# Padding four small tiles so that every operand on chip begins at a multiple of 128 bytes

## The chip, the cores and the metric

The kernel runs on one core of a Trainium2 chip. The metric is the device time of one execution in microseconds (us). A time for a kernel is the median of several executions. The profile is one further execution, recorded by the hardware profiler.

## The reference

```python
X = np.fft.rfft(x, axis=1)                    # x: 8 x 3008 x 256, float32
Yr = Xr @ w_r - Xi @ w_i + b_r                # 256 x 256 complex projection
Yi = Xr @ w_i + Xi @ w_r + b_i
Yr = np.sign(Yr) * np.maximum(np.abs(Yr) - 0.01, 0.0)      # and Yi the same
y = np.fft.irfft(Yr + 1j * Yi, n=3008, axis=1).astype(np.float32)
h = y.reshape(24064, 256) @ w_in              # 256 x 2048
out = np.maximum(0.01 * h, h) @ w_out         # 2048 x 256, result float32
```

Two parts follow each other: a spectral layer (Fourier transform, complex projection, soft threshold, inverse transform) and an MLP over 24064 tokens with a leaky ReLU between its two matrix products.

## The kernel before

**Transform.** The sequence length 3008 is 47 x 64, and the transform is done in two steps of matmuls, a 47-point one (`fwd`, `stage_a`, 120 partitions: 24 folded rows times 5 groups) and a 64-point one (`mid`, `stage_b`). Between them the data goes through a scratch tensor in HBM (`u_dram`), since the second step wants it in another layout. `proj` multiplies by the complex weights with three real products (`wr`, `wd`, `wn`), thresholds, and `stage_g` transforms back over 64 points. The result goes through HBM again (`v_dram`), and `inverse` does the last 47-point step with the constant `ga` and puts 512 tokens at a time into a tile `yc`.

**MLP.** 47 chunks `ci` of 512 tokens, and in each 8 steps `q` over the hidden width. The first product is done by Strassen's scheme with seven block products instead of eight: `forms` makes the seven token combinations (`yh`, `yl`, seven slots of 256 columns), and the weights' seven combinations lie in `win` (7 x 8 blocks of 128 columns). Each block product is three matmuls in float32r (`block`, L92), since every operand is split into a high and a low part: high x high, low x high, high x low. `moe_a` and `moe_b` combine the products in PSUM, apply the leaky ReLU into `gf`, and split that into `gh` and `gl`; `moe_o` (L576) makes the second product, 512 columns wide, from the stationary `wout` and the moving `gh`, `gl`.

The stationary operand of a matmul is loaded by a LDWEIGHTS, the moving one streams through. In L92 the stationary operand is `win` and the moving one `yh` or `yl`. In `proj` (L78) the stationary operand is the data `eh` and the moving one a weight (`wr`, `wd`, `wn`). In `stage_b` (L343) the data `u` is stationary and the constant `fb` moves; in `inverse` (L480) the data `vin` is stationary and the constant `ga` moves.

**Order.** A scheduler lays out the order of each engine. The transform of the next sequence is interleaved with the MLP of the present one at a pace that the code sets (`Stream`). Batch 0 and the loading of the weights form a start phase of about 170 us.

**Where tiles lie.** On chip memory has 224 KB in each partition. Tiles are placed one behind the other, constants first (`fb`, `sign`, then the pairs made by `pair`, then `bias`, `ga`), then the working tiles of the pool `sb` by their tag. A tile's start is thus the sum of the sizes ahead of it, rounded to 32 bytes. Added up for the kernel before:

| tile | first byte | its rest modulo 128 |
|---|---|---|
| `fb` | 1152 | 0 |
| `sign` (36 columns, 144 bytes) | 7552 | 0 |
| `win_hi`, `win_lo` | 7712, 36384 | 32 |
| `wr`, `wd`, `wn`, `gb` (hi and lo) | 65056 to 77856 | 32 |
| `fa0_hi`, `fa0_lo`, `fa1_hi`, `fa1_lo` (480 bytes each) | 78368 to 79808 | 32, 0, 96, 64 |
| `bias`, `ga`, `xi` (and `fa32`, 1440 bytes, in the same place) | 80288, 82336, 83360 | 32 |
| `yl`, `yh`, `gf`, `gl`, `gh`, `yc`, `wout`, `eh`, `zh`, `u`, `v`, `vin`, `xin`, `kc`, `t`, `ob` | 84800 to 220480 | 64 |
| `odd` (960 bytes) | 222528 | 64 |
| `p1`, `u2` | 223488, 224512, 225536 | 0 |

Slots inside the tiles of the MLP are 512 or 1024 bytes apart, so each operand of the MLP has the rest of its tile.

Of the kernel before, what the change touches and what calls it, by code (L numbers as in the profile page):

```python
# [8 lines left out]
F32 = mybir.dt.float32  # L9
F32R = mybir.dt.float32r  # L10
# [8 lines left out]
N1, N2, NK1 = 47, 64, 24  # L19
NG, NS = 5, 13  # L20
P = 128
PA = NK1 * NG
# [8 lines left out]
def spectral_mlp_kernel(  # L31
# [22 lines left out]
    NPAIR = NK1 // 2  # L54
# [8 lines left out]
    const = ctx.enter_context(tc.tile_pool(name="const", bufs=1))  # L63
    sb = ctx.enter_context(tc.tile_pool(name="sb", bufs=2))
# [4 lines left out]
    def bank(tag, bufs):  # L69
        return ps.tile([P, 512], F32, name=tag, tag=tag, bufs=bufs)  # L70
# [27 lines left out]
    consts = {}  # L98

    def pair(name, shape):  # L100
        consts[name] = tuple(const.tile(shape, F32R, name=f"{name}_{p}") for p in ("hi", "lo"))
        return consts[name]

    def load_plain(name, src, shape):
# [3 lines left out]
    def split_consts():  # L108
        for name in ("wr", "wd", "wn", "gb", "fa0", "fa1"):
            w = consts[name + "32"][0]  # L110
            hi, lo = pair(name, list(w.shape))
            act.copy(hi, w)
            dve.tensor_sub(lo, w, hi.bitcast(F32))
# [354 lines left out]
    def inverse(pi, eh):  # L468


        (_, _, n0), (_, _, n1) = pairs[pi]
        m = n0 + n1
        ne, n = m * NK1, m * N1
        vin = v_t[pi]
        py = bank("psf", 2)
        s = slice(eh * P, (eh + 1) * P)
        for c in range(2):
            for i in range(2):
                o = c * ne + i * n0 * NK1
                nc.tensor.matmul(py[:, o:o + P], vin[:, c, i, s], consts["ga"][:, c, :], start=True, stop=True)  # L480
        odd = sb.tile([P, 2 * NG * NK1], F32, name="odd", tag="odd", bufs=1)[:, :ne]
        y = sb.tile([P, NT], F32, name="y", tag="y")
        act.copy(odd, py[:, ne:2 * ne])
        dve.tensor_add(y[:, :ne], py[:, :ne], odd)
        ev, ov = (t.rearrange("p (m k) -> p m k", k=NK1)[:, :, 1:] for t in (py[:, :ne], odd))
        dve.tensor_sub(y[:, ne:n].rearrange("p (m k) -> p m k", m=m), ev, ov)
        lo = p0[pi]
        while lo < p0[pi + 1]:
            ci = lo // NT
            hi = min((ci + 1) * NT, p0[pi + 1])  # L490
            if ci not in f_t:
                f_t[ci] = sb.tile([P, NH, NT], F32, name="yc", tag="yc")
            act.copy(f_t[ci][:, eh, lo - ci * NT:hi - ci * NT], y[:, lo - p0[pi]:hi - p0[pi]])
            lo = hi
# [98 lines left out]
    def tokens(ci):  # L593

        yield
        for p in due[ci]:
            v_load(p)
            yield
        for _ in range(4 - len(due[ci])):
            yield  # L600
        for eh in range(NH):
            for p in due[ci]:
                inverse(p, eh)
                yield
        yield from forms(ci)
# [39 lines left out]
    FWD = NS * 6 * D  # L645


    fa32 = sb.tile([PA, 3, PA], F32, name="fa32", tag="xi", bufs=1)
    for h in range(2):
        sync.dma_start(fa32[:, h], fa[h])  # L650
    for h in range(3):
# [8 lines left out]
    for p in (0, 32):  # L660
        for r, src in enumerate((b_r, b_i)):
            sync.dma_start(brow[p:p + 1, r * D:(r + 1) * D], src.unsqueeze(0))
    sign = const.tile([P, NK1 + NPAIR], F32, name="sign")
    sync.dma_start(sign, sg)
    sync.dma_start(consts["gb32"][0], gb)

# [4 lines left out]
    f0.finish()  # L671
    load_win(1, (sync, sync), written[7])
    pair("win", [P, 7, NQ, P])
    win_tmp = (
        sb.tile([P, NH * NIN], F32, name="cva", tag="vin"), sb.tile([P, NH * NIN], F32, name="cvq", tag="gf"),
# [33 lines left out]
    for eh in range(NH):  # L709
        for p in due[0]:  # L710
            inverse(p, eh)
# [131 lines left out]
```

## Time and profile before

| | |
|---|---|
| time of the kernel, median of 3 runs | 2604.93 us (2601.47 to 2607.09) |
| time of the profiled execution | 2600.34 us |
| its span, first to last instruction | 2598.6 us |
| TensorE matmul busy | 2537.5 us (98%) |
| VectorE, ScalarE, GpSimd busy | 1897.1 us (73%), 1668.5 us (64%), 229.6 us (9%) |
| mean granted TensorE clock | 0.993 |

PE is TensorE's matmul stream, PEld its weight loads, DVE VectorE, ACT ScalarE, POOL GpSimd. Matmuls overlap each other in the records: a matmul with 256 columns is shown 280 ns long while the next one starts about 117 ns after it. So the pace of TensorE is read from the starts, and durations serve to compare like with like.

### The profile page before, as it was taken

To read this page: it belongs to the slowest core of one execution; us is meant where nothing else is said; L and a number is where in the kernel's file an instruction comes from. 1 tells how busy PE (TensorE), PEld (TensorE's weight loads), DVE (VectorE), ACT (ScalarE), POOL (GpSimd) and SP (SyncE) were. 2 spreads that over 40 slices of the span, in tenths; PEclk is the share of its full clock that TensorE was granted. 3 is DMA by queue.
4 is the path that set the end of the run, shared out by engine and by line. 5 is a ranking of instruction groups with operands and counts; after the bars stand their busy time and mean duration, and the time that the engine had idled before them with its cause. 6 is when DMAs were issued, how large, how long until landed. Compare 5 with 4: busy or idle time off the path is not lost.

```text
span 2598.6 us, 42643 instructions
## 1 busy us (share of the span) xinstructions
PE 2537.5 (98%) x16300; PEld 2281.5 (88%) x16300; DVE 1897.1 (73%) x3403; ACT 1668.5 (64%) x3174; POOL 229.6 (9%) x180
## 2 busy tenths in 40 slices
PE   5999999999999999999999999999999999999999
PEld 4689888999889998899988999889998889999998
DVE  7687786776777778777786777877777777767675
ACT  5766665776556666567665666566666667655564
POOL 0001121100110001100021000210002000000000
PEclk8999999999999999999999999999999999999999
DMA  8621132111221113211132111321113221101000
GB/s 259 179 85 50 48 89 72 54 47 48 82 78 49 45 41 90 75 55 51 33 97 68 49 49 37 104 67 49 49 36 101 64 58 48 44 17 32 9 17 17
DMA packets 119912, 165.13 MB, mean 64 GB/s; under 512 B 13601, under 2 KB 69917, under 8 KB 119709
## 3 DMA queue, kind: packets, MB, share of 16 engines
q1 hardware_dynamic: 79120, 115.55, 14.6%
q10 hardware_dynamic: 40589, 46.87, 7.1%
q8 instruction: 128, 2.10, 0.4%
q14 instruction: 75, 0.61, 0.1%
HBM read 86.60 MB, written 75.76 MB: 62 GB/s over the span
## 4 chain that ended last, share of the span: by engine, by line
PE 89%; DVE 3%; DMA 2%; ACT 1%; issue 0%; ACTq 0%; SPq 0%; DVEq 0%
PE pso L576 38%; PE psh L92 34%; PE psf L78 11%; PE psf L480 3%; PE psf L343 3%; DMA u<-u_dram 1%; DMA u_dram<-xin 1%; DVE yl L506 0%; DVE gl L563 0%; DMA raw<-w_out_dram 0%; DVE gf L557 0%; ACT gh L561 0%; DVE yt L511 0%; ACT gf L559 0%; DVE yc L512 0%
## 5 line engine op out<-in xcount | busy, mean ns | idle before, releaser
L92 PE MATMUL psh<-yh,win_hi 128*128 128x256 f32 x2632 | 752.3, 286 | 13.8 <-DVE gf L546 10.6
L92 PE MATMUL psh<-yl,win_hi 128*128 128x256 f32 x2632 | 738.3, 280 | 0.6 <-DVE yl L506 0.5
L92 PE MATMUL psh<-yh,win_lo 128*128 128x256 f32 x2632 | 737.9, 280 | 0.0
L576 PE MATMUL pso<-gh,wout_hi 128*128 128x512 f32 x1504 | 593.9, 395 | 0.0
L576 PE MATMUL pso<-gl,wout_hi 128*128 128x512 f32 x1504 | 591.1, 393 | 0.5 <-DVE gl L563 0.5
L576 PE MATMUL pso<-gh,wout_lo 128*128 128x512 f32 x1504 | 590.4, 393 | 0.0
L563 DVE TENSOR_TENSOR gl<-gf,gh 128x1024 fp32r<-128x1024 f32 x376 | 471.8, 1255 | 92.7 <-ACT gh L561 90.6
L92 PEld LDWEIGHTS psh<-yh,win_hi 128*128 128x128 f32 x2632 | 497.0, 189 | 30.7 <-DVE gf L546 15.4
L92 PEld LDWEIGHTS psh<-yl,win_hi 128*128 128x128 f32 x2632 | 497.0, 189 | 12.5 <-DVE yl L506 1.0
L92 PEld LDWEIGHTS psh<-yh,win_lo 128*128 128x128 f32 x2632 | 496.6, 189 | 0.2
L557 DVE TENSOR_TENSOR gf<-psh,u 128x512 f32<-128x512 f32 x376 | 259.1, 689 | 256.3 <-PE psh L92 255.1
L561 ACT CAST gh<-gf 128x1024 fp32r<-128x1024 f32 x376 | 396.4, 1054 | 7.1
L559 ACT ACTIVATE gf<-gf 128x768 f32<-128x768 f32 x376 | 320.0, 851 | 49.5 <-DVE gf L557 47.7
L576 PEld LDWEIGHTS pso<-gl,wout_hi 128*128 128x128 f32 x1504 | 282.5, 188 | 62.9 <-DVE gl L563 1.0
L576 PEld LDWEIGHTS pso<-gh,wout_hi 128*128 128x128 f32 x1504 | 283.1, 188 | 46.9 <-ACT gh L561 0.4
L576 PEld LDWEIGHTS pso<-gh,wout_lo 128*128 128x128 f32 x1504 | 282.9, 188 | 44.9
L556 ACT ACTIVATE gf<-psh 128x256 f32<-128x256 f32 x376 | 145.5, 387 | 266.6 <-PE psh L92 246.9
L542 ACT COPY p<-psh 128x256 f32<-128x256 f32 x376 | 140.1, 373 | 220.2 <-PE psh L92 219.1
L379 POOL TENSOR_TENSOR kb<-bias,kc 128x512 f32<-128x512 f32 x84 | 119.0, 1417 | 1530.6 <-ACT kc L376 1409.6
L543 DVE TENSOR_TENSOR u<-psh,p 128x256 f32<-128x256 f32 x376 | 158.6, 422 | 105.8 <-ACT p L542 103.5
L545 DVE TENSOR_TENSOR gf<-psh,u 128x256 f32<-128x256 f32 x376 | 159.3, 424 | 29.7 <-PE psh L92 2.0
L546 DVE TENSOR_TENSOR gf<-psh,gf 128x256 f32<-128x256 f32 x376 | 159.1, 423 | 9.0
(134 smaller groups left out, 3253.2 us busy)
## 6 DMA issues: line engine op xcount, KB each, us to landing
u<-u_dram SPq DMA_DIRECT2D x192, 128.0 KB, 2.7
v_dram<-v ACTq DMA_DIRECT2D x192, 128.0 KB, 2.4
out_dram<-ob SPq DMA_DIRECT2D x94, 256.0 KB, 2.1
vin<-v_dram SPq DMA_DIRECT2D x96, 240.0 KB, 3.5
xin<-x_dram SPq DMA_DIRECT2D x90, 240.0 KB, 3.0
u_dram<-xin ACTq DMA_DIRECT2D x72, 240.0 KB, 2.4
u_dram<-xin SPq DMA_DIRECT2D x24, 240.0 KB, 3.9
raw<-w_out_dram SPq DMA_DIRECT2D x8, 512.0 KB, 5.0
```

The source lines that it names most:

```text
L78: last = nc.tensor.matmul(dst, a, b, start=(i == 0), stop=(i == len(terms) - 1))
L92: mlp[:] = [nc.tensor.matmul(dst, a, b, start=start and i == 0, stop=i == 2, skip_group_check=True)]
L542: act.copy(p1, b1[:, lo])
L543: dve.tensor_add(u2, b1[:, hi], p1)
L545: dve.tensor_add(g[:, 3], b2[:, hi], u2)
L546: dve.tensor_add(g[:, 3], b2[:, lo], g[:, 3])
L556: act.activation(g[:, 0], b1[:, lo], AF.Prelu, alpha=SLOPE)
L557: dve.tensor_add(g[:, 1:3], b2.rearrange("p (k n) -> p k n", k=2), u2.unsqueeze(1).broadcast_to([P, 2, HT]))
L559: act.activation(g[:, 1:4], g[:, 1:4], AF.Prelu, alpha=SLOPE)
L561: cp = act.copy(gh, g)
L563: parted[:] = [cp, dve.tensor_sub(gl, g, gh.bitcast(F32))]
L576: mlp[:] = [nc.tensor.matmul(po, a[:, f, s], r[:, i], start=(f == 0 and j == 0), stop=(f == NF - 1 and j == 2),)]
```

## The change

Four tiles whose row is no multiple of 128 bytes are made longer, and the code uses only the first part of each: the split constants made by `pair` (of which only the four `fa` tiles change, from 120 to 128 columns), `odd` (240 to 256 columns), `fa32` (rows of 120 to rows of 128) and `sign` (36 to 64 columns).

```diff
     def pair(name, shape):
-        consts[name] = tuple(const.tile(shape, F32R, name=f"{name}_{p}") for p in ("hi", "lo"))
+        full = shape[:-1] + [-(-shape[-1] // 32) * 32]
+        consts[name] = tuple(
+            const.tile(full, F32R, name=f"{name}_{p}")[..., :shape[-1]] for p in ("hi", "lo"))
         return consts[name]
...
-        odd = sb.tile([P, 2 * NG * NK1], F32, name="odd", tag="odd", bufs=1)[:, :ne]
+        odd = sb.tile([P, 256], F32, name="odd", tag="odd", bufs=1)[:, :ne]
...
-    fa32 = sb.tile([PA, 3, PA], F32, name="fa32", tag="xi", bufs=1)
+    fa32 = sb.tile([PA, 3, P], F32, name="fa32", tag="xi", bufs=1)[:, :, :PA]
...
-    sign = const.tile([P, NK1 + NPAIR], F32, name="sign")
+    sign = const.tile([P, 64], F32, name="sign")[:, :NK1 + NPAIR]
```

Everything behind a lengthened tile moves up: `win` to `gb` by 96 bytes, `bias`, `ga` and `xi` by 224, the working tiles by 320, `p1` and `u2` by 384. Afterwards every tile that the code allocates begins at a multiple of 128 bytes, and all of them but `sign` at 128 bytes past a multiple of 512 (before: `win` 32, `yh`, `gh` and `wout` 320, `p1` and `u2` 256 past one). Instructions, their order on each of the five engines and their semaphore waits are the same before and after, row by row; only source lines shift by three.

## The prediction

> **What bounds the kernel now.** I read the page first: busy times, the clock and the chain of work that ended last.
>
> ```profile
> span 2598.6 us, 42643 instructions
> PE 2537.5 (98%) x16300; PEld 2281.5 (88%) x16300; DVE 1897.1 (73%) x3403; ACT 1668.5 (64%) x3174; POOL 229.6 (9%) x180
> ...
> PE 89%; DVE 3%; DMA 2%; ACT 1%; issue 0%; ACTq 0%; SPq 0%; DVEq 0%
> PE pso L576 38%; PE psh L92 34%; PE psf L78 11%; PE psf L480 3%; PE psf L343 3%; DMA u<-u_dram 1%; DMA u_dram<-xin 1%; DVE yl L506 0%; DVE gl L563 0%; DMA raw<-w_out_dram 0%; DVE gf L557 0%; ACT gh L561 0%; DVE yt L511 0%; ACT gf L559 0%; DVE yc L512 0%
> ```
>
> TensorE is nearly always busy, and 89% of the chain is its own work. DVE, ACT and DMA together hold 6%. Second, the busy times by stage, to see whether that is an average over unlike stages (the columns are PE, PEld, DVE, ACT, POOL, then clock, DMA share and GB/s):
>
> ```profile
> 0.00:65.00 65.00, 38.28 (x149) 26.98 (x150) 47.38 (x80) 33.49 (x60) 0.52 (x5) 0.84 0.84 259
> 170.00:2330.00 2160.00, 2139.03 (x14023) 1946.99 (x14023) 1593.77 (x2868) 1410.54 (x2708) 228.73 (x174) 1.00 0.21 59
> ```
>
> From 170 us to 2330 us, 83% of the span, PE is busy 99% of the time at the full granted clock, with DMA at 0.21 of its capacity. Only the first 65 us are a matter of DMA (0.84 busy). So a layout change matters through one thing above all: how long TensorE takes per matmul. The groups by shape say how many there are:
>
> ```profile
> L92 PE MATMUL psh<-yh,win_hi 128*128 128x256 f32 x2632 | 752.3, 286 | 13.8 <-DVE gf L546 10.6 <-DVE u L543 3.0
> L92 PE MATMUL psh<-yl,win_hi 128*128 128x256 f32 x2632 | 738.3, 280 | 0.6 <-DVE yl L506 0.5
> L92 PE MATMUL psh<-yh,win_lo 128*128 128x256 f32 x2632 | 737.9, 280 | 0.0
> L576 PE MATMUL pso<-gh,wout_hi 128*128 128x512 f32 x1504 | 593.9, 395 | 0.0
> L576 PE MATMUL pso<-gl,wout_hi 128*128 128x512 f32 x1504 | 591.1, 393 | 0.5 <-DVE gl L563 0.5
> L576 PE MATMUL pso<-gh,wout_lo 128*128 128x512 f32 x1504 | 590.4, 393 | 0.0
> ```
>
> That makes 3 x 2632 = 7896 matmuls of 256 columns and 3 x 1504 = 4512 of 512 columns in the MLP. The durations overlap each other, so the pace comes from the starts in the timeline. The first three lines below are one stretch, the next two a second, the last four a third:
>
> ```profile
> 1004.75 0.28 PE L92 MATMUL psh<-yh,win_hi 128*128 128x256 f32 x1
> ...
> 1006.49 0.40 PE L576 MATMUL pso<-gh,wout_hi 128*128 128x512 f32 x1
> ...
> 1009.24 0.63 PE L78 MATMUL psf<-xz,fa_hi 120*120 120x512 f32 x2
> ...
> 456.83 0.28 PE L78 MATMUL psf<-wn_hi,eh 128*128 128x256 f32 x1
> ...
> 458.25 1.05 PE L343 MATMUL psf<-fb,u 128*128 128x128 f32 x8
> ...
> 13.84 1.02 PE L78 MATMUL psh<-xin,fa 120*120 120x512 f32 x2
> 14.70 1.02 PE L78 MATMUL psh<-xs,fa 120*120 120x512 f32 x2
> ...
> 22.12 0.59 PE L78 MATMUL psh<-xs,fa 120*120 120x256 f32 x2
> 22.55 0.59 PE L78 MATMUL psh<-xin,fa 120*120 120x256 f32 x2
> ```
>
> Fifteen L92 matmuls start from 1004.75 on and before 1006.49: 1.74 / 15 = 0.116 us each. Twelve of L576 between 1006.49 and 1009.24: 2.75 / 12 = 0.229 us. Twelve of the projection between 456.83 and 458.25: 1.42 / 12 = 0.118 us. The plain float32 ones of the start take 0.86 / 2 = 0.430 us for 512 columns and 0.43 / 2 = 0.215 us for 256.
>
> **The change part by part.** No instruction is added, removed, resized or moved, and no wait changes. So there are no instructions to cost; each term is a number of existing instructions times whatever their duration changes when their operands start elsewhere. Before, operands start 0, 32, 64 and 96 bytes past a multiple of 128, so the profile already holds the comparison, in pairs of equal shape:
>
> ```profile
> L92 PEld LDWEIGHTS psh<-yh,win_lo 128*128 128x128 f32 x2632 | 496.6, 189 | 0.2
> L576 PEld LDWEIGHTS pso<-gh,wout_lo 128*128 128x128 f32 x1504 | 282.9, 188 | 44.9
> L78 PEld LDWEIGHTS psf<-xz,fa_hi 120*120 120x120 f32 x168 | 30.0, 182 | 4.3
> L78 PEld LDWEIGHTS psf<-xz,fa_lo 120*120 120x120 f32 x84 | 15.3, 182 | 3.8
> L78 PE MATMUL psf<-wn_lo,eh 128*128 128x256 f32 x168 | 47.2, 281 | 0.0
> L78 PE MATMUL psf<-zh,gb_lo 128*128 128x512 f32 x84 | 33.2, 395 | 0.0
> L480 PE MATMUL psf<-ga,vin 120*128 120x128 f32 x832 | 114.2, 275 | 0.0
> L343 PE MATMUL psf<-fb,u 128*128 128x128 f32 x672 | 93.9, 275 | 9.6 <-DMA u<-u_dram 9.6
> L542 ACT COPY p<-psh 128x256 f32<-128x256 f32 x376 | 140.1, 373 | 220.2 <-PE psh L92 219.1
> L376 ACT COPY kc<-psf 128x256 f32<-128x256 f32 x84 | 31.2, 372 | 21.4 <-PE psf L78 13.6 <-DMA v_dram<-v 4.4 <-ACT gf L556 1.7
> L354 ACT COPY xi<-psf 128x256 f32<-128x256 f32 x84 | 31.2, 372 | 57.8 <-PE psf L343 57.1
> L543 DVE TENSOR_TENSOR u<-psh,p 128x256 f32<-128x256 f32 x376 | 158.6, 422 | 105.8 <-ACT p L542 103.5
> L546 DVE TENSOR_TENSOR gf<-psh,gf 128x256 f32<-128x256 f32 x376 | 159.1, 423 | 9.0
> ```
>
> *Weight loads.* `win` starts at 32, `wout` at 64: 189 and 188 ns. `fa_hi` mixes 32 and 96, `fa_lo` 0 and 64: 182 and 182 ns, and two of the four already sit where the change puts everything, or half way. I take 0 for all 12408 loads of the MLP.
>
> *Moving operands in float32r.* `yh` and `yl` start at 64 (280 ns, pace 0.116 us), the projection's weights at 32 (281 ns, pace 0.118 us). For 512 columns, `gh` with `wout` 393 to 395 ns, `zh` with `gb` 395 ns. So moving from an odd multiple of 32 to one of 64 is worth 1 ns or nothing; the step from 64 to 128 isn't shown for float32r. It is shown for plain float32: `ga` at 32 and `fb` at 0 take 275 ns both. I take 0. As the end on the gain side I give the unseen step the 1 ns of the seen one, on the 7896: 7.9 us less. Nothing excludes a loss, since the relative places of `win` and `yh` change as well, so the other end is 7.9 us more.
>
> *ACT and DVE.* `p1` (shown as p) at 0, `kc` at 64, `xi` at 32: 373, 372 and 372 ns. `u2` (shown as u, with its input p) at 0 and `gf` at 64: 422 and 423 ns. No difference above 1 ns in 372, so 0.3% of the 4% of the chain that they hold, 104 us: 0.3 us either way. I take 0; what else they do hides behind a PE that is busy 99%, and were that cover gone, 1 ns on each of the 3403 + 3174 instructions would still be only 6.6 us.
>
> *DMA.* Rows keep their number and size. All tiles that big transfers read or fill move from 64 to 128 past a multiple of 256. The typical issues:
>
> ```profile
> u<-u_dram SPq DMA_DIRECT2D x192, 128.0 KB, 2.7
> v_dram<-v ACTq DMA_DIRECT2D x192, 128.0 KB, 2.4
> out_dram<-ob SPq DMA_DIRECT2D x94, 256.0 KB, 2.1
> ```
>
> No pair in the trace compares two starts for a transfer of one size and direction. The nearest bound is what the direction is worth at equal size, 2.7 against 2.4 us, 11%. On the 2% of the chain that is DMA, 52 us, that is 5.8 us either way. I take 0, because twice the bytes (`ob`) land in 2.1 us: these times are mostly not bytes, and an effect of the start could touch only the bytes. The Trainium skill ("DMA: Bandwidth & Descriptors", section "How a descriptor splits into AXI transactions") has a rule that speaks against this change: a read may begin only at a multiple of 256 bytes, and the bytes between that multiple and the start are fetched and dropped. By it a row of 2048 bytes would cost 68 beats instead of 66 when read out of the new places, 3% more, and on the 1% of the chain that is `u_dram<-xin` (26 us) this is 0.8 us, an estimate from that page: the sum would be +0.8 instead of 0. No row here shows it.
>
> *The padding itself.* `fa` and `fa32` are used through the same 120 columns, `odd` and `sign` through theirs; 384 bytes more of space cost no time.
>
> The sum is 0. The profiled execution took 2600.34 us (1.7 us around its span of 2598.6) and 2600.34 + 0 stays 2600.34; it was 4.6 us below the median of the runs, 2604.93. Since I compare medians, the forecast is 2604.9 us.
>
> **The rivals.**
>
> *No effect* (the forecast): 2604.9 us.
>
> *Whole lines of 128 bytes for the moving operand: much faster.* Before, every float32r moving operand starts off a multiple of 128, so a cost that all of them pay would be invisible in the pairs above. Something of that kind may exist: half of the plain float32 pace is 0.215 us for 512 columns and 0.1075 us for 256, while float32r takes 0.229 and 0.116. If that excess came from the start, the gain would be 4512 x 0.014 + 7896 x 0.0085 = 63 + 67 = 130 us, giving 2475 us. Against it: 32 and 64 pay the same, and an excess of 14 against 8.5 ns grows with the columns, where one extra line at the start would cost the same for any length. That half of float32's pace is the floor of float32r is itself not shown.
>
> *A small gain of the same kind,* the 1 ns per matmul above: 2597 us. For it there is one pair, 281 against 280, within the spread of the rows (280 to 286).
>
> *Weights and moving operand at the same place modulo 512: slower.* In L92 `win` (32 past a multiple of 512) and `yh` (320) differ now; afterwards both are at 128. If two streams read by TensorE at once disturbed each other where their places agree, L92 would slow down. At 1 ns on each of 7896 it would be 2613 us, and it decides from 5.2 / 7896 = 0.66 ns. Against it: `wout` and `gh` agree already (both 320), and they run at 393 to 395 ns, while `gb` (32) with `zh` (320) takes 395.
>
> *The change doesn't reach the operands:* not so here, since all slots in the MLP are 512 or 1024 bytes apart; it would also give 2604.9.
>
> **How the numbers follow.** No effect 0.82; lines of 128 bytes 0.05; the small gain 0.05; the same place 0.05; DMA at its slow bound (2604.9 + 5.8 = 2611) 0.03. This measurement tells about 0.2%, 5.2 us, from no change; the three runs shown spread over 5.6 us. Faster is 0.05 + 0.05, slower 0.05 + 0.03, same 0.82. The range is the largest single bound, 7.9 us, on either side: 2597 to 2613. It holds all cases but the large gain.
>
> **What would show it.** In the changed kernel's groups, right is: L92 at 280 to 286 ns and L576 at 393 to 395 ns, starts 0.116 and 0.229 us apart, LDWEIGHTS at 188 to 189, L542 at 373. Wrong by the first rival: starts of L92 near 0.108 us and of L576 near 0.215. Wrong by the last: L92 slower while L576 stays. DMA would show in `u<-u_dram` off its 2.7 us and `ob` off 2.1. If the time moves with none of these rows moving, the cause is a wait, and then the idle time of PE before L92 (13.8 us now) must have grown.

## The result: 0.6% slower, in TensorE's pace

| | before | changed |
|---|---|---|
| time, median | 2603.45 us (2601.47 to 2607.09) | 2620.34 us (2618.45 to 2621.34) |
| ratio | | 1.0062, 95% interval 1.0045 to 1.0080 |
| profiled execution, span | 2600.34 us, 2598.6 us | 2621.34 us, 2619.6 us |

The forecast was no change, 2604.9 us, and the range ended at 2613. The page of the changed kernel has the same number of instructions; PE is 20.8 us longer busy, DVE and ACT are within about 2 us of before.

```profile
span 2619.6 us, 42643 instructions
PE 2558.3 (98%) x16300; PEld 2303.9 (88%) x16300; DVE 1898.9 (72%) x3403; ACT 1666.4 (64%) x3174; POOL 228.8 (9%) x180
```

The groups of the changed kernel (mean ns after the bar's busy time):

```profile
L92 PE MATMUL psh<-yh,win_hi 128*128 128x256 f32 x2632 | 758.9, 288 | 13.9 <-DVE gf L549 10.3
L92 PE MATMUL psh<-yl,win_hi 128*128 128x256 f32 x2632 | 746.7, 284 | 0.6 <-DVE yl L509 0.5
L92 PE MATMUL psh<-yh,win_lo 128*128 128x256 f32 x2632 | 746.8, 284 | 0.0
L579 PE MATMUL pso<-gh,wout_hi 128*128 128x512 f32 x1504 | 595.6, 396 | 0.0
L579 PE MATMUL pso<-gh,wout_lo 128*128 128x512 f32 x1504 | 591.2, 393 | 0.0
L579 PE MATMUL pso<-gl,wout_hi 128*128 128x512 f32 x1504 | 587.7, 391 | 0.5 <-DVE gl L566 0.5
L92 PEld LDWEIGHTS psh<-yh,win_lo 128*128 128x128 f32 x2632 | 504.2, 192 | 0.2
L545 ACT COPY p<-psh 128x256 f32<-128x256 f32 x376 | 139.9, 372 | 230.7 <-PE psh L92 229.0
L546 DVE TENSOR_TENSOR u<-psh,p 128x256 f32<-128x256 f32 x376 | 158.7, 422 | 109.9 <-ACT p L545 106.6
L549 DVE TENSOR_TENSOR gf<-psh,gf 128x256 f32<-128x256 f32 x376 | 159.0, 423 | 9.0
```

The three L92 groups went from 286, 280 and 280 ns to 288, 284 and 284, their weight loads from 189 to 192. L579 (L576 before) has 396, 393 and 391 ns where 395, 393 and 393 stood. ACT and DVE have the durations of before within 1 ns. PE's idle time before L92, 13.9 us, was 13.8: no wait appeared. The transfers didn't move either:

```profile
u<-u_dram SPq DMA_DIRECT2D x192, 128.0 KB, 2.7
v_dram<-v ACTq DMA_DIRECT2D x192, 128.0 KB, 2.4
out_dram<-ob SPq DMA_DIRECT2D x94, 256.0 KB, 2.1
```

The timeline of the changed kernel (start, duration, engine) shows the pace. Twenty L92 matmuls start from 1006.45 on and before 1008.85:

```profile
1006.45 0.28 PE L92 MATMUL psh<-yl,win_hi 128*128 128x256 f32 x1
...
1008.85 0.40 PE L579 MATMUL pso<-gh,wout_hi 128*128 128x512 f32 x1
```

2.40 / 20 = 0.120 us, where it was 0.116. For the whole execution I took every pair of following PE starts that begins with an L92 matmul, left out pairs over 130 ns apart (a change of partner or a wait lies between), and averaged: 117.1 ns before, 119.6 now, over some 7650 pairs each. 7896 x 2.5 = 19.7 us. The same average for the 512-column matmuls (pairs under 255 ns) is 230.1 and 229.7: 1.8 us less. Together 17.9 us, against 16.9 between the medians and 21.0 between the two spans. The spans contain one more thing. The 609th matmul starts at 170.1 us in the profiled execution before and at 174.4 in that of the changed kernel. This is the start phase, which varies: in the profiled executions of the fifteen whole kernels of this document the moment lies between 169.9 and 175.4 us, and not in the order of L92's pace (169.9 in e5_d128 with 119.3 ns, 175.4 in e7_d32 with 118.2 ns). From there to the last matmul the changed kernel loses another 16.7 us: the intervals that begin with an L92 matmul grow by 17.2 us in all, everything else shrinks by 0.5. So behind the start phase the loss lies in L92.

A count that needs no choice of pairs: the matmuls that fit between 170 and 2330 us (first bracket of the row), 14023 before.

```profile
170.00:2330.00 2160.00, 2140.09 (x13930) 1951.65 (x13929) 1587.74 (x2858) 1401.95 (x2699) 228.00 (x174) 1.00 0.21 59
```

14023 / 13930 = 1.0067, near the ratio of the times.

### The profile page after: what moved, and what is told of

Its sections match the earlier page's. It is cut to its first block, busy times and chain, and to the rows that moved or that the text cites. A ratio compares the mean times of both kernels' runs of the same rounds, so it can differ in the third digit from the quotient of the medians.

```text
span 2619.6 us, 42643 instructions
## 1 busy us (share of the span) xinstructions
PE 2558.3 (98%) x16300; PEld 2303.9 (88%) x16300; DVE 1898.9 (72%) x3403; ACT 1666.4 (64%) x3174; POOL 228.8 (9%) x180
## 3 DMA queue, kind: packets, MB, share of 16 engines
q1 hardware_dynamic: 79120, 115.55, 14.4%
## 4 chain that ended last, share of the span: by engine, by line
PE 89%; DVE 2%; DMA 2%; ACT 1%; issue 0%; ACTq 0%; SPq 0%; DVEq 0%
PE pso L579 37%; PE psh L92 35%; PE psf L78 11%; PE psf L483 3%; PE psf L346 3%; DMA u<-u_dram 1%; DMA u_dram<-xin 1%; DVE yl L509 0%; DVE gl L566 0%; DMA raw<-w_out_dram 0%; ACT gh L564 0%; DVE gf L560 0%; ACT gf L562 0%; DVE yc L515 0%; DVE yt L514 0%
## 5 line engine op out<-in xcount | busy, mean ns | idle before, releaser
L92 PE MATMUL psh<-yh,win_hi 128*128 128x256 f32 x2632 | 758.9, 288 | 13.9 <-DVE gf L549 10.3
L92 PE MATMUL psh<-yl,win_hi 128*128 128x256 f32 x2632 | 746.7, 284 | 0.6 <-DVE yl L509 0.5
L92 PE MATMUL psh<-yh,win_lo 128*128 128x256 f32 x2632 | 746.8, 284 | 0.0
L579 PE MATMUL pso<-gh,wout_hi 128*128 128x512 f32 x1504 | 595.6, 396 | 0.0
L579 PE MATMUL pso<-gh,wout_lo 128*128 128x512 f32 x1504 | 591.2, 393 | 0.0
L579 PE MATMUL pso<-gl,wout_hi 128*128 128x512 f32 x1504 | 587.7, 391 | 0.5 <-DVE gl L566 0.5
L92 PEld LDWEIGHTS psh<-yh,win_hi 128*128 128x128 f32 x2632 | 504.3, 192 | 30.9 <-DVE gf L549 14.9
L92 PEld LDWEIGHTS psh<-yl,win_hi 128*128 128x128 f32 x2632 | 504.6, 192 | 11.2 <-DVE yl L509 1.0
L92 PEld LDWEIGHTS psh<-yh,win_lo 128*128 128x128 f32 x2632 | 504.2, 192 | 0.2
L579 PEld LDWEIGHTS pso<-gl,wout_hi 128*128 128x128 f32 x1504 | 283.1, 188 | 62.5 <-DVE gl L566 1.0
L579 PEld LDWEIGHTS pso<-gh,wout_hi 128*128 128x128 f32 x1504 | 284.6, 189 | 47.5 <-ACT gh L564 0.4
L579 PEld LDWEIGHTS pso<-gh,wout_lo 128*128 128x128 f32 x1504 | 284.6, 189 | 42.8
L382 POOL TENSOR_TENSOR kb<-bias,kc 128x512 f32<-128x512 f32 x84 | 118.6, 1411 | 1545.0 <-ACT kc L379 1426.8
```

Of the source, the lines that this page charges most:

```text
L92: mlp[:] = [nc.tensor.matmul(dst, a, b, start=start and i == 0, stop=i == 2, skip_group_check=True)]
L579: mlp[:] = [nc.tensor.matmul(po, a[:, f, s], r[:, i], start=(f == 0 and j == 0), stop=(f == NF - 1 and j == 2),)]
```

## Experiments

I call *distance* the place of the stationary operand minus that of the streamed one, in bytes modulo 256. In L92 it is `win` minus `yh` (`yl` lies like `yh`): 224 before, 0 in the changed kernel. In L576 it is `wout` minus `gh`: 0 in both. Unless said otherwise, the experiments have the instructions, order and waits of before.

### Which operand, and absolute or relative

**e1_win**: only the constants move.

```diff
-    sign = const.tile([P, NK1 + NPAIR], F32, name="sign")
+    sign = const.tile([P, 64], F32, name="sign")[:, :NK1 + NPAIR]
...
-        load_plain("ga", ga, [PA, 2, P])
+        consts["ga"] = const.tile([PA, 2 * P + 104], F32, name="ga")[:, :2 * P].rearrange("p (a b) -> p a b", a=2)
+        sync.dma_start(consts["ga"], ga)
```

> Only the weights' side is moved: win, wr, wd, wn, gb start where the change puts them (128 past a multiple of 512), yh, yl, gh, gl, wout and all other working tiles keep the place of before (320). Three theories of the 17 us. Same place: L92 is slow when win and yh start at the same place modulo 512; here they are 192 apart, so L92 starts 117.1 ns apart, its weight loads take 189 ns, about 2604 us. Aligned moving operand: L92 is slow when yh starts at a multiple of 128; here it doesn't, so 2604 us as well. Aligned weights: slow when win starts at a multiple of 128; here it does, so 119.6 ns, loads 192 ns, about 2620 us.

Measured: 2593.6 us, ratio to before 0.9964 (0.9951 to 0.9977): faster than both kernels, which no theory had. L92 starts 116.3 ns apart, loads take 189 ns. Its recorded durations are those of before (286, 280 and 280 ns): the gain shows in the starts alone. The same stretch as above holds more matmuls than in either kernel, 14023 / 14087 = 0.9955:

```profile
170.00:2330.00 2160.00, 2138.74 (x14087) 1947.19 (x14086) 1601.09 (x2882) 1412.98 (x2719) 229.27 (x174) 1.00 0.21 59
```

**e2_work**: only the working tiles move (the kernel before, `odd` of 256 columns, `ga` lengthened by 80 columns).

> Only the working tiles are moved: yh, yl, gh, gl, wout, p1, u2 start where the change puts them (128 past a multiple of 512), win, wr, wd, wn, gb keep the place of before (32). Same place: win and yh are 96 apart, so L92 stays at 117.1 ns and 189 ns for a load, about 2604 us. Aligned moving operand: yh is a multiple of 128, so 119.6 ns, about 2620 us. Aligned weights: win is not, so 117.1 ns, about 2604 us.

Measured: 2621.9 us, 1.0071 (1.0056 to 1.0086), L92 119.6 ns, loads 189 ns: as slow as the changed kernel without its longer loads. By itself this speaks for the aligned streamed operand.

**e3_both320**: both at 320 past a multiple of 512 (`sign` of 112 columns, `ga` lengthened by 56).

> win and yh start at the same place modulo 512, but at none that is a multiple of 128 (both 320 past a multiple of 512, 64 past a multiple of 128). Same place: L92 is slow as in the changed kernel, 119.6 ns, loads 192 ns, about 2620 us. Aligned moving operand and aligned weights: neither is aligned, so 117.1 ns, 189 ns and about 2604 us.

Measured: 2619.4 us, 1.0064 (1.0049 to 1.0079), L92 119.6 ns, loads 192 ns. Nothing of L92 is aligned to 128 here, and it is as slow as in the changed kernel. Alignment of the one or the other is out.

**e4_apart256**: the changed kernel with `ga` lengthened by 64 columns, so that all working tiles move by 256 bytes.

> The changed kernel with all working tiles 256 bytes further: every operand still starts at a multiple of 128, but win is at 128 and yh at 384 past a multiple of 512. Same place modulo 512: L92 fast again, 117.1 ns, loads 189 ns, about 2604 us (if the modulus were 256 or 128 it would stay slow). Aligned moving operand and aligned weights: still 119.6 ns and about 2620 us.

Measured: 2620.32 us, 1.0065 (1.0049 to 1.0082), L92 119.6 ns. So not modulo 512: the changed kernel, e3 and e4 share the distance 0 modulo 256, and agree in L92's pace and in the time. Here are L92 and its loads in e3_both320, to be set beside the rows of the changed kernel above:

```profile
L92 PE MATMUL psh<-yl,win_hi 128*128 128x256 f32 x2632 | 746.8, 284 | 0.6 <-DVE yl L506 0.5
L92 PEld LDWEIGHTS psh<-yh,win_lo 128*128 128x128 f32 x2632 | 504.3, 192 | 0.2
```

What remained was the distance. But e2_work (distance 160) was slow where "the same place" had promised 2604, so zero is not the only bad value.

### The other distances

**e5_d128, e6_d192, e7_d32**: e1_win with `ga` lengthened by 24, 8 and 48 columns instead of 104.

> So far the distance from yh up to win decides, wherever both lie: 0 modulo 128 gave 2620 us in three kernels, 32 gave 2622, 64 gave 2594, 96 (the kernel before) 2603. Here win is at 128 and yh at 0 past a multiple of 512: distance 128. If the pattern repeats every 128 bytes: as at 0, L92 starts 119.6 ns apart, about 2620 us. If it repeats every 256 bytes only, 128 is a new value, half a period from 0, and should be far from it: 117 ns or less, 2604 us or less.

> win at 128, yh at 448 past a multiple of 512: distance 192 modulo 256, 64 modulo 128. Repeats every 128: as at 64, L92 at 116.6 ns, about 2594 us. Repeats every 256 only: a new value, a quarter period from 128 and from 0, between 2594 and 2622 us.

> win at 128, yh at 96 past a multiple of 512: distance 32 modulo 256. Repeats every 128: as at 160, L92 at 119.9 ns, about 2622 us. Repeats every 256 only: a new value, between the 2620 of 0 and the 2594 of 64, about 2607 us.

Measured: 2614.7 us, 1.0041 (1.0026 to 1.0056), L92 119.3 ns for distance 128; 2595.81 us, 0.9974 (0.9962 to 0.9986), 116.8 ns for 192; 2609.46 us, 1.0027 (1.0018 to 1.0036), 118.2 ns for 32. 0 with 128 and 64 with 192 are near each other, but 32 (118.2 ns) and 160 (119.6 ns) are not: the pattern resembles itself after 128 bytes and isn't the same. That 256 is the period is shown directly at distance 0 alone, by e4_apart256; in the kernel no other distance was run 256 bytes further.

### The second product

**e8_wout64, e10_wout32, e11_wout96**: e1_win with `wout` 16, 8 and 24 elements further than `gh`.

```diff
-            sb.tile([P, NF, D], F32R, name=f"wout_{p}", tag=f"wout_{p}", bufs=1) for p in ("hi", "lo"))
+            sb.tile([P, NF * D + 128], F32R, name=f"wout_{p}", tag=f"wout_{p}", bufs=1)[:, 16:16 + NF * D]
+            .rearrange("p (a f) -> p a f", a=NF) for p in ("hi", "lo"))
```

> The fast kernel with win 64 past yh modulo 128, and besides wout moved 64 bytes up against gh and gl (distance 64 instead of 0), so that the matmuls of 512 columns are shifted too. If the distance acts on every float32r matmul as it does in the few of zh with gb (231 ns between starts at distance 0, 235 at 64), the 4512 of L579 (here L576) go from 230 to 234 ns, 18 us more: about 2612 us. If only matmuls of 256 columns feel it: L576 stays at 230 ns and the time at 2594 us. If 64 is good for both: below 2590 us.

Measured: 2598.4 us, 0.9985 (0.9976 to 0.9995). The 512-column matmuls went from 229.6 to 233.0 ns: 15 us lost, near the 18 expected. (The pair behind the expectation, `zh` with `gb`, was counted modulo 128. In e1_win it lies at 192 modulo 256, so that the size came out is in part luck.) The time was expected at 2612, since L92 was to stay, but L92 gained a further 1 ns (115.3).

```profile
L577 PE MATMUL pso<-gh,wout_hi 128*128 128x512 f32 x1504 | 598.0, 398 | 0.0
L577 PE MATMUL pso<-gl,wout_hi 128*128 128x512 f32 x1504 | 595.5, 396 | 0.5 <-DVE gl L564 0.5
```

The starts show where L92's gain comes from. Its matmuls come in runs, mostly of some twenty, between other matmuls, and at distance 64 a run keeps one of two paces. Of the 366 runs of e1_win with at least nine intervals, 159 average under 115.5 ns (114.1 in the mean) and 205 over 116.5 ns (117.8); two lie between. In e8_wout64, 238 are fast and 125 slow. Most of the difference is in the runs that follow directly on a matmul of `wout`: 21 of 127 are fast in e1_win, 119 of 127 here. One such run, at the same place of the program, first in e1_win, then in e8_wout64 (first and last of 21 matmuls):

```profile
285.24 0.28 PE L92 MATMUL psh<-yh,win_hi 128*128 128x256 f32 x1
...
287.59 0.28 PE L92 MATMUL psh<-yh,win_lo 128*128 128x256 f32 x1
...
285.51 0.28 PE L92 MATMUL psh<-yh,win_hi 128*128 128x256 f32 x1
...
287.79 0.28 PE L92 MATMUL psh<-yh,win_lo 128*128 128x256 f32 x1
```

2.35 / 20 = 0.1175 us against 2.28 / 20 = 0.114. Modulo 256 only `wout` has moved between the two kernels. So the operands of the matmul ahead have a part in which pace a run takes; how, no run shows.

> The fast kernel (win 64 past yh modulo 128) with wout 32 bytes up against gh and gl. The 512-column matmuls took 229.6 ns at distance 0 and 233.0 at 64. If 0 is their best, 32 lies between: 231 to 232.5 ns, 2600 to 2607 us. If their best is elsewhere: below 229.6 ns and below 2594 us.

> The same with wout 96 bytes up. If 0 is the best distance for 512 columns: 231 to 233 ns, 2600 to 2609 us. If their best is at 96: below 229.6 ns and below 2594 us.

Measured: 233.3 ns and 2605.9 us, 1.0017 (1.0007 to 1.0028); 233.7 ns and 2611.7 us, 1.0039 (1.0025 to 1.0054). Both paces are slower than was expected (at most 232.5 and 233 ns). For 512 columns the best of the four distances is 0, where 256 columns are slow. Of the runs of L92 behind a `wout` matmul 66 of 128 are fast with `wout` at 32, and 6 of 129 at 96.

### One of three operands

**e9_yl64**: the changed kernel, `yl` alone 64 bytes further.

```diff
-        yh, yl = y_t[ci] = tuple(sb.tile([P, 7, HT], F32R, name=n_, tag=n_) for n_ in ("yh", "yl"))
+        yh = sb.tile([P, 7, HT], F32R, name="yh", tag="yh")
+        yl = sb.tile([P, 7 * HT + 128], F32R, name="yl", tag="yl")[:, 16:16 + 7 * HT].rearrange("p (k n) -> p k n", k=7)
+        y_t[ci] = (yh, yl)
```

> The changed kernel with yl alone 64 bytes further, so that of the three matmuls of a product the second (yl) streams at distance 64 from win modulo 128, the first and third (yh) at distance 0. If the distance acts between the streamed operand and the weight load that runs beside it, only the interval that begins with the yl matmul gets shorter, to about 116 ns, and the other two stay at 119.6: L92 at 118.4 on average, 2632 x 3.3 ns = 9 us less than the changed kernel, about 2611 us. If it is a matter of the kernel's whole layout (which buffers lie where), all three intervals or none move: 2594 or 2620 us.

Measured: 2613.38 us, 1.0049 (1.0034 to 1.0064), L92 118.2 ns on average. The size was right, the place was not: the three kinds of interval (pairs inside a run of L92) take 118.2, 118.6 and 117.8 ns, where the changed kernel has 119.3, 119.6 and 119.8. (As counted here, modulo 256, this `yl` lies at distance 192.) So the interval isn't set by the pair of operands in it alone; the stream as a whole settles into a rhythm, that is, into a pace that all its intervals share.

### TensorE alone

**e12_stream**: no transform and no MLP, only streams of matmuls in L92's groups of three, from tiles that ACT and DVE filled once; every stream has another distance. There is one execution of it. The names s_a to s_p are 256 columns at 0, 16, ... 240, l_a to l_p 512 columns.

```python
def run(name, n, dw, dy=(0, 0)):
    banks = [ps.tile([P, 512], F32, name=name, tag="bank") for _ in range(2)]
    slots = 7 if n == 256 else 3
    for q in range(NQ):
        for k in range(slots):
            dst = banks[k % 2][:, :n]
            s = k * NQ + q
            for i, (a, b) in enumerate(((0, 0), (0, 1), (1, 0))):
                nc.tensor.matmul(dst, wat(a, s, dw), yat(b, k, n, dy[b]), start=(i == 0), stop=(i == 2))
```

> TensorE alone: no transform, no MLP, no work of DVE, ACT or GpSimd beside it, only streams of matmuls in groups of three as in L92, once at 256 columns (126 in a stream) and once at 512 (54), with the stationary operand 0, 16, ... 240 bytes further than the moving one (names s_a to s_p and l_a to l_p); the output is zeros. If two reads of TensorE disturb each other, the pace follows the whole kernels: 256 columns about 119.6 ns at 0 and 128, 118 to 120 at 32 and 160, 116.5 at 64 and 192, 117.1 at 224; 512 columns 229.7 at 0, 233 to 234 at 32, 64 and 96. Both operands 64 bytes up (s_both) equals s_a, and ylo alone 64 up (s_ylo) lies between s_a and 64 (s_e or s_m). If the disturbance comes from other engines' accesses, the pace is the same at all 16 distances and below 116 ns.

The groups of this run (the time of a stream is the busy time less its last matmul, over the others):

```profile
L44 PE MATMUL s_a<-y,w 128*128 128x256 f32 x126 | 15.3, 283 | 0.0
L44 PE MATMUL s_both<-y,w 128*128 128x256 f32 x126 | 15.3, 283 | 0.0
L44 PEld LDWEIGHTS s_a<-y,w 128*128 128x128 f32 x126 | 15.2, 192 | 0.0
L44 PE MATMUL s_ylo<-y,w 128*128 128x256 f32 x126 | 15.0, 278 | 0.0
L44 PE MATMUL s_o<-y,w 128*128 128x256 f32 x126 | 14.9, 279 | 0.0
L44 PE MATMUL s_e<-y,w 128*128 128x256 f32 x126 | 14.4, 276 | 0.0
L44 PEld LDWEIGHTS s_e<-y,w 128*128 128x128 f32 x126 | 14.4, 188 | 0.0
L44 PE MATMUL l_e<-y,w 128*128 128x512 f32 x54 | 12.8, 395 | 0.0
L44 PE MATMUL l_a<-y,w 128*128 128x512 f32 x54 | 12.4, 389 | 0.0
```

s_a: (15.3 - 0.283) / 125 = 0.120 us; s_e, at 64: (14.4 - 0.276) / 125 = 0.113; l_a: (12.4 - 0.389) / 53 = 0.227; l_e: 0.234. The 192 ns of the loads at distance 0 are there as well, and s_both (both operands 64 bytes up) is s_a. DVE and ACT have nothing to do beside these streams: their last instruction ends at 24 us, before the first stream of the list (s_a, at 41 us). A transfer of zeros to the output still runs until about 72 us, beside s_a and s_b; s_again, distance 0 once more at 309 us without it, takes 119.9 ns, s_a 120.0. So it is TensorE with itself. In s_ylo one of the three matmuls lies at distance 192 and two at 0, and all three kinds of interval take 117.5 to 118.2 ns, the pace of a stream wholly at 192: as in e9_yl64, the intervals share one pace. The means of all starts, beside those of the whole kernels:

| distance | L92 in the kernel, ns | 256 columns alone, ns | `wout` in the kernel, ns | 512 columns alone, ns |
|---|---|---|---|---|
| 0 | 119.6 (changed, e3, e4) | 120.0 | 229.7 (changed) | 227.2 |
| 32 | 118.2 (e7) | 118.3 | 233.3 (e10) | 233.2 |
| 64 | 116.3 (e1) | 113.4 | 233.0 (e8) | 233.2 |
| 96 | not run | 117.3 | 233.7 (e11) | 234.1 |
| 128 | 119.3 (e5) | 118.7 | | 233.4 |
| 160 | 119.6 (e2) | 120.0 | | 233.4 |
| 192 | 116.8 (e6) | 117.8 | | 229.1 |
| 224 | 117.1 (before) | 116.7 | | 233.3 |

L92 follows the streams within 1 ns, except at 64, where its runs have the two paces told above, 114.1 and 117.8 ns, and the stream only the fast one.

### Other lengths, and the rest of the kernel

**e13_all**: e1_win with a gap of 128 bytes ahead of `wr` and of 64 ahead of `gb`, the pairs padded as in the change, `ga` lengthened by 24 columns. **e1_again**: e1_win, on the same chip.

> The fast kernel e1_win, with the other float32r matmuls at the best distance that the streams alone showed: the projection's eh 64 past its weights (was 192), gb and fa at 0 from zh and xz (were 64 and mixed). If what the streams of TensorE alone show holds for each kind of matmul in the whole kernel: the 1512 of the projection go from 117.6 to about 115.5 ns (3 us), the 468 of 512 columns from 233 to about 228 ns (2 us), 5 us less than e1_win, 2589 us. If only the MLP feels it: equal to e1_win, 2594 us.

> e1_win once more, on the same chip as e13_all, to compare the two closely: 0.9964 of the time before, about 2594 us.

Measured: e13_all 2593.4 us, 0.9968 (0.9957 to 0.9979); e1_again 2595.14 us, 0.9975 (0.9966 to 0.9984). The intervals overlap. The projection went from 117.5 to 117.3 ns only, `gb` from 233.2 to 230.8, `fa` not down. The 5 us didn't come. The pace of a long stream doesn't carry over to the short runs of these matmuls; why not was not tried.

**e14_lengths**: streams alone at seven lengths and four distances; a to d are 0, 64, 128, 192.

> Streams of TensorE alone as in e12_stream, at 128, 192, 256, 320, 384, 448 and 512 columns (nc_ to ni_) and at distances 0, 64, 128, 192 (a to d); the output is zeros. At 256 columns again 120.0, 113.4, 118.6, 117.8 ns and at 512 227.2, 233.2, 233.4, 229.2. If each matmul must wait for one weight load and a load takes as long as 256 columns, 128 and 192 columns run no faster than about 110 ns, and distance matters only where load and stream run side by side all the time. If the best distance goes with where the stream stands when the load begins, it changes with the length, and 320 to 448 have bests of their own; if there is one best distance per kernel, it is 64 or 0 for all.

```profile
L44 PE MATMUL nc_a<-y,w 128*128 128x128 f32 x126 | 14.2, 274 | 0.0
L44 PE MATMUL nc_c<-y,w 128*128 128x128 f32 x126 | 14.2, 275 | 0.0
L44 PE MATMUL ne_a<-y,w 128*128 128x256 f32 x126 | 15.3, 283 | 0.0
L44 PE MATMUL ne_b<-y,w 128*128 128x256 f32 x126 | 15.0, 281 | 0.0
L44 PE MATMUL nf_a<-y,w 128*128 128x320 f32 x54 | 8.1, 309 | 0.0
L44 PE MATMUL nf_c<-y,w 128*128 128x320 f32 x54 | 8.1, 308 | 0.0
L44 PE MATMUL ng_b<-y,w 128*128 128x384 f32 x54 | 9.7, 338 | 0.0
L44 PE MATMUL ng_d<-y,w 128*128 128x384 f32 x54 | 9.5, 336 | 0.0
```

128 and 192 columns take 111.3 to 111.9 ns (means of starts) at every distance. So there is a floor that doesn't depend on the columns, and on it the distance has no effect; the weight load that each matmul has is the nearest explanation, but no stream without loads was run. 320 columns take 146.6 to 146.7 at every distance; 384 take 173.3 to 176.7, 448 take 200.0 to 203.9, 512 take 226.7 to 233.4. From 320 on the lowest values lie on a line, about 26.7 ns for 64 columns, on which 256 columns would take 120.0, their worst; at 256 some distances get below it. So the best distance does go with the length, as the one theory had it, but not at all lengths. And ne_b, 256 columns at distance 64, was expected at the 113.4 ns of s_e in e12_stream, the same operands, and took 117.8: these are the two paces that the runs of L92 have side by side in e1_win. One distance allows more than one rhythm. The stream ahead was at distance 0 here and at 48 there, and the two ran on different chips; which of these decided wasn't tried.

## Why the prediction was wrong

*What bounds the kernel* held: only TensorE's time per matmul mattered, and behind the start phase the loss is there.

*The step that failed* is the one on moving operands in float32r. It read the start of each operand by itself, from pairs (`yh` at 64, 280 ns; the projection's weights at 32, 281 ns), and took 0. Those pairs had different distances from their stationary partner: 224 in L92, and in the projection, where `eh` (320) is stationary and the weight (32) streams, 288, which is 32 modulo 256. The prediction's own starts, 0.116 against 0.118 us, held 2 ns between these two; it priced the step by the durations, 280 against 281 ns, at 1 ns or nothing. What the change altered was the distance of `win` from `yh`, 224 to 0, and that costs 2.5 ns on each of 7896, 19.7 us where the sum has 0. e3_both320 and e4_apart256 show that the start by itself does nothing, so the rival of a small gain falls too.

*Weight loads* were taken at 0 by the same reading; they went from 189 to 192 ns, because of the distance (192 in e3 too, 189 in e1_win with the aligned `win`). The longer loads are not what costs the time: e2_work has 189 ns and the same loss.

*The rival "same place: slower"* had the right place, sign and kind, at a chance of 0.05 and a price of 1 ns where 2.5 was measured. I turned it down with `wout` and `gh`, which lie at distance 0 and run well. The streams show why that was no counterexample: at 512 columns 0 is among the best distances, at 256 among the worst. An observation on one length was carried to another. Its modulus, 512, was wrong as well: e4 lies 256 apart and is as slow.

*The rival "whole lines of 128 bytes"* is out: with every operand on a multiple of 128, L92 is slower.

*ACT, DVE and DMA* came out as costed, 0: 372, 422 and 423 ns, and 2.7, 2.4 and 2.1 us for the transfers. The rule of the Trainium skill ("DMA: Bandwidth & Descriptors", section "How a descriptor splits into AXI transactions") on reads that begin off a multiple of 256 bytes had 0.8 us at stake. Of `u_dram<-xin`, the 72 issues from ACT stayed at 2.4 us. The 24 from SP (the sync engine's queue) went from 3.9 to 4.3, but that isn't the place: they take 3.8 to 4.4 us in kernels that leave these tiles where they were (e1_again, e10_wout32) and 3.8 in e9_yl64, where they lie as in the change. An effect of 3% can't be told from that.

The Trainium skill ("SBUF — State Buffer", section "Who interferes with whom") gives TensorE two independent read ports, one for the streamed operand and one for the weight load, and says that it never waits on anyone. The runs agree for other engines: L92's pace is the same whether DVE and ACT are busy or idle beside it (before, 117.3 ns over the pairs with both under 10% busy and 117.1 over those with both over 90%). For TensorE's own two reads the independence doesn't show in the pace: e12_stream moves one of them against the other and changes the pace by 6.6 ns in 120. That the two reads collide is the nearest explanation; the runs show the dependence on the distance, not the collision itself.

## What to carry to other kernels

Where TensorE is the bound and every float32r matmul loads its own weights, the place of the stationary operand against the streamed one, modulo 256 bytes, can matter: up to 6% of the pace in streams alone (113.4 against 120.0 ns at 256 columns), 1% of the time in this kernel. It is free to choose: here 1.0062 against 0.9964 of the time, from 96 bytes on one small tile and a pad that keeps the rest in place. Aligning everything puts all pairs at distance 0, which was among the best at 512 columns and among the worst at 256; measure a stream alone at the kernel's own length, as in e12_stream, before choosing, and then the kernel, since its short runs needn't take the pace of the stream. To judge such a change from a profile, compare starts, not durations, and compare pairs of operands, not operands.

## What the runs showed of the hardware

- A float32r stream of 256 columns, one weight load each, takes 113.4 to 120.0 ns a matmul by the distance alone; 512 columns 226.7 to 234.1; 128, 192 and 320 columns don't depend on it at the four distances run.
- One distance can have two paces: at 64 the runs of L92 in e1_win take 114.1 or 117.8 ns, and the matmul ahead has a part in which (21 fast runs of 127 behind `wout` at distance 0, 119 of 127 behind `wout` at 64).
- With a load per matmul there is a floor of 111.3 to 111.9 ns, at 128 columns as at 192.
- At distance 0, the recorded duration of a load is 192 ns instead of 187 to 189 in 256-column streams, at each place of the operands that was run (s_a, s_both).
